# Attention and a cosine-gated feed-forward on one core: the second product for two batches at a time by Strassen's scheme

## The chip, the cores and the metric

The kernel runs on one core of one Trainium2 chip. The metric is the device time of one execution in microseconds (us); shown is the median of several runs. One execution was also taken by the hardware profiler, and all the views of the profile below come from that one.

## The reference

```
q_n, k_n = rmsnorm(q, g_q), rmsnorm(k, g_k)
scores = q_n @ k_n^T / sqrt(64)
attn = softmax(scores)                     # 8 batches, 12 heads, 448 x 448
x = (attn @ v) as 3584 tokens x 768        # 448 tokens of each batch
h = x @ w_in                               # 768 -> 2048
g = h * cos(h)
out = g @ w_out                            # 2048 -> 768
```

Everything is float32 but the two weights, which arrive as float64 and are turned into float32 on the chip. Products are taken at more than the precision of one pass: each operand is split into a high part that TensorE's fast 32-bit format holds (`F32R`) and a low part, the rest, and a product is hi*hi + hi*lo + lo*hi, three matmuls.

## The kernel before

All work is cut into small parts: a Python function that issues a few instructions on one engine. `Plan.add` records a part with its engine, an assumed cost, a due time and the keys it reads and writes; `Plan.order` simulates the five engines' queues with these costs, picks on each engine the ready part with the earliest due time, and so writes out one fixed order. On the chip each engine works through its own instructions in that order and waits on semaphores for the others. There are two plans, one behind the other.

**The first plan** holds the attention of all 8 batches (6 pairs of heads each), the first product (`ffn1`, L478) of batches 0 to 6 laid between, and the decoding of both weights. The first product writes h to DRAM (`h_out` L497, `h_store` L501). The second weight is handled by `weights2` (L606) in 32 halves of 128 x 384: fetched by SP (`v_fetch`), turned from float64 by four instructions of VectorE and one of ScalarE (`decode`, L204), split into high part (ScalarE, L256) and low part (GpSimd, L258), and stored to the scratch tensor `wo_d` in DRAM (`v_store`).

**The second plan** (from L737) has two kinds of work for TensorE. First come the 16 blocks of batch 7's first product (`ffn1_block`), each of 18 matmuls. As each of them ends, the slot of its weight in SBUF takes one row block of the second weight (`v_place`, L265). Then comes the second product of batches 0 to 7 (`ffn2`, L548): 16 steps a batch, a step being one row block of 128 of w_out for six output tiles of 128 x 448, so 6 x 3 = 18 matmuls of 128 x 128 by 128 x 448. The six outputs of a batch build up in six of the eight banks of PSUM.

The operand g of the second product is made for two row blocks at a time, as tiles of 128 x 896 floats, 8 groups a batch and 64 in all. For each of them

- SP loads h from DRAM (`gl_load`, L509),
- VectorE counts turns, h/2pi + a rounding constant (L516), and GpSimd makes the multiple to be subtracted (L518),
- VectorE reduces h in two steps (L524, L526),
- ScalarE takes the absolute value and the sine (L530, L531),
- VectorE multiplies by h (L535),
- ScalarE casts the high part (L544), and GpSimd subtracts it to get the low part (L542).

All their operands lie in SBUF. The rings of buffers are 4 (h), 2 (turns), 2 (reduced), 3 and 3 (high and low parts). At the end of a batch, ScalarE and VectorE copy the six outputs out of PSUM in turn (L568, L570), and SP stores them (`y_store`, L572).

The heart of the second product is

```
nc.tensor.matmul(y, whi, hi, start=(fc == 0), stop=False)
nc.tensor.matmul(y, whi, lo, start=False, stop=False)
nc.tensor.matmul(y, wlo, hi, start=False, stop=(fc == NFC - 1))
```

Of the kernel before, what the change touches and what calls it, by code (L numbers as in the profile page):

```python
# [126 lines left out]
def tile_attention_moe(  # L127
# [108 lines left out]
    half = {}  # L236

    def v_fetch(fc, hf):
        cs = slice(hf * HM, hf * HM + HM)
        st = apool.tile([128, DM], I32, tag="wf", name=f"rawo{fc}_{hf}", bufs=RING["wf"])  # L240
        f = apool.tile([128, DM], F32, tag="wf", name=f"wo{fc}_{hf}", bufs=RING["wf"])
        half[(fc, hf)] = (st, f[:, :HM])
        if f64:
            nc.sync.dma_start(st, w_out[fc][:, cs].bitcast(I32))
        else:
            nc.sync.dma_start(f[:, :HM], w_out[fc][:, cs])

    def v_decode(fc, hf, step):
        st, f = half[(fc, hf)]
        if f64:  # L250
            decode(st, f, step)

    def v_split(fc, hf, lo):
        st, f = half[(fc, hf)]
        if not lo:
            nc.scalar.copy(st.bitcast(F32R)[:, :HM], f)  # L256
        else:
            nc.gpsimd.tensor_tensor(st.bitcast(F32R)[:, HM:], f, st.bitcast(F32)[:, :HM], ALU.subtract)  # L258
# [246 lines left out]
    gts = {}  # L505

    def gl_load(b, gi):
        hb = gpool.tile([128, NG, S], F32, tag="hb", name=f"hb{b}_{gi}", bufs=4)
        nc.sync.dma_start(hb, h_d[b, gi * NG : gi * NG + NG].rearrange("f p s -> p f s"))  # L509
        gts[(b, gi)] = {"h": hb}  # L510

    def g_turns(b, gi, step):
        d = gts[(b, gi)]
        if step == 0:
            n = d["n"] = gpool.tile([128, NG, S], F32, tag="n", name=f"n{b}_{gi}", bufs=2)
            nc.vector.tensor_scalar(n, d["h"], 1.0 / (2.0 * math.pi), MAGIC, op0=ALU.mult, op1=ALU.add)  # L516
        else:
            nc.gpsimd.tensor_scalar(d["n"], d["n"], -MAGIC, -C1, op0=ALU.add, op1=ALU.mult)  # L518

    def g_reduce(b, gi, step):  # L520
        d = gts[(b, gi)]
        if step == 0:
# [1 line left out]
            nc.vector.tensor_tensor(r, d["h"], d["n"], ALU.add)  # L524
        else:
            nc.vector.scalar_tensor_tensor(d["r"], d.pop("n"), C2 / C1, d["r"], op0=ALU.mult, op1=ALU.add)  # L526

    def g_cos(b, gi):
        r = gts[(b, gi)]["r"]
        nc.scalar.activation(r, r, AF.Abs)  # L530
        nc.scalar.activation(r, r, AF.Sin, bias=halfpi, scale=-1.0)  # L531

    def g_mul(b, gi):
        d = gts[(b, gi)]
        nc.vector.tensor_tensor(d["r"], d["r"], d.pop("h"), ALU.mult)  # L535

    def g_split(b, gi, lo):
        d = gts[(b, gi)]
        t = gpool.tile([128, NG, S], F32R, tag="glo" if lo else "ghi", name=f"g{lo}{b}_{gi}")
        d["lo" if lo else "hi"] = t  # L540
        if lo:
            nc.gpsimd.tensor_tensor(t, d.pop("r"), d["hi"].bitcast(F32), ALU.subtract)  # L542
        else:
            nc.scalar.copy(t, d["r"])  # L544

    ys = {}

    def ffn2(b, fc):  # L548
        d = gts[(b, fc // NG)]
        hi, lo = d["hi"][:, fc % NG, :], d["lo"][:, fc % NG, :]  # L550
        w = wts[("wo", fc)]
        for oc in range(NOC):
            if fc == 0:
                ys[(b, oc)] = ps_y.tile([128, 512], F32, tag="y", name=f"y{b}_{oc}")
            y = ys[(b, oc)][:, :S]
            whi = w[:, 0, oc * 128 : oc * 128 + 128]
            wlo = w[:, 1, oc * 128 : oc * 128 + 128]
            nc.tensor.matmul(y, whi, hi, start=(fc == 0), stop=False)  # L558
            nc.tensor.matmul(y, whi, lo, start=False, stop=False)  # L559
            nc.tensor.matmul(y, wlo, hi, start=False, stop=(fc == NFC - 1))  # L560

    yes = {}

    def y_out(b, oc):
        y = ys.pop((b, oc))[:, :S]
        ye = yes[(b, oc)] = xpool.tile([128, S], F32, tag=f"xf{oc}", name=f"ye{b}_{oc}")
        if oc % 2 == 0:
            nc.scalar.copy(ye, y)  # L568
# [37 lines left out]
    def weights2(fc, hf):  # L606
        i = 2 * fc + hf
        d = base(2 * NP) + i * (base(NU - NP // 2) - base(2 * NP)) / (2.0 * NFC)
        st, f = ("wf", NFC + 2 * i), ("wf", NFC + 2 * i + 1)
        add(SP, ISS, d - 20.0, v_fetch, fc, hf, w=[st, f], land=LAND, start=d - 30.0)  # L610
        if f64:
            for step, eng, cost in ((0, DVE, 0.42), (1, DVE, 0.7), (2, DVE, 0.7), (3, ACT, 0.56), (4, DVE, 0.66)):
                add(eng, cost, d + step, v_decode, fc, hf, step,
                    r=[st] if step != 3 else [], w=[f] if step != 3 else [st])
        add(ACT, 0.5, d + 8.0, v_split, fc, hf, False, r=[f], w=[st])
        add(POOL, 1.0, d + 10.0, v_split, fc, hf, True, r=[f], w=[st])
        add(SP, ISS, d + 14.0, v_store, fc, hf, r=[st], land=LAND)
# [119 lines left out]
    RING2 = {"he": 2, "hb": 4, "n": 2, "r2": 2, "ghi": 3, "glo": 3, "y": 8}  # L737
    gpool = ctx.enter_context(tc.tile_pool(name="gpool", bufs=3, reuse_waits="tile"))
    ps_y = ctx.enter_context(tc.tile_pool(name="ps_y", bufs=8, space=PSUM, reuse_waits="tile"))
# [10 lines left out]
    for b in range(B):  # L750
        for gi in range(NFC // NG):
            n = (NFC // NG) * b + gi
            d = BLOCK * (NFC * (b + 1) + NG * gi)
            hb, t, r2, hi, lo = (("hb", n), ("n", n), ("r2", n), ("ghi", n), ("glo", n))
            add(SP, ISS, d - 30.0, gl_load, b, gi, r=[("hd", b, NG * gi + i) for i in range(NG)], w=[hb], land=LAND)
            add(DVE, 0.9, d - 20.0, g_turns, b, gi, 0, r=[hb], w=[t])
            add(POOL, 1.3, d - 19.0, g_turns, b, gi, 1, w=[t])
            add(DVE, 1.1, d - 17.0, g_reduce, b, gi, 0, r=[hb, t], w=[r2])
            add(DVE, 1.8, d - 16.0, g_reduce, b, gi, 1, r=[t], w=[r2])
            add(ACT, 2.0, d - 14.0, g_cos, b, gi, w=[r2])  # L760
            add(DVE, 1.12, d - 11.0, g_mul, b, gi, r=[hb], w=[r2])
            add(ACT, 0.95, d - 9.0, g_split, b, gi, 0, r=[r2], w=[hi])
            add(POOL, 2.8, d - 8.0, g_split, b, gi, 1, r=[r2, hi], w=[lo])
# [58 lines left out]
```

## Time and profile before

| What | us |
|---|---|
| median of 3 runs | 1551.31 (1550.73 to 1553.91) |
| span of the profiled execution, first to last instruction | 1548.5 |
| TensorE busy in it | 1458.9 |
| VectorE busy | 1071.5 |
| ScalarE busy | 884.5 |
| GpSimd busy | 878.3 |

The page gives the span of the profiled execution, and the runs' times include what lies around a span: the median is 2.8 us above it. PE is TensorE's matmuls, PEld its weight loads, DVE VectorE, ACT ScalarE, POOL GpSimd and SP the queue that issues the DMAs. A row of a group gives line, engine, operation, output and inputs, shape and count, then the busy time in us and the mean duration in ns, then the idle time of the engine in front of these instructions and what ended it. Matmuls are pipelined: one shows some 365 ns from start to end, but the next starts 0.2 us behind it, and their busy time counts overlapping ones once. Time in which an instruction waits for a shared resource after it has started counts as busy.

### The profile page before, as it was taken

Reading aid. Unit: us, or ns where it says so; the run is one execution under the profiler, and the core shown is the slowest. Engines: PE = TensorE matmul, PEld = TensorE weight load, DVE = VectorE, ACT = ScalarE, POOL = GpSimd, SP = SyncE. Lnnn points to the kernel's source line nnn. Section 1 sums busy time; section 2 is a strip of 40 time slices with the busy share of each in tenths; the row PEclk is TensorE's granted clock in tenths of the full one; section 3 lists DMA queues with packets and bytes.
Section 4 is the critical chain, followed back from the end, with each engine's and each line's share of the span. In section 5 each row is a group of like instructions: output and inputs, shape, how many; then the busy total and the mean of one; then the engine's idle time right before and its main releaser. Section 6 shows DMA issues by size and latency. Waiting matters only on the chain.

```text
span 1548.5 us, 22570 instructions
## 1 busy us (share of the span) xinstructions
PE 1458.9 (94%) x7680; PEld 1236.1 (80%) x7680; DVE 1071.5 (69%) x1915; ACT 884.5 (57%) x1786; POOL 878.3 (57%) x727
## 2 busy tenths in 40 slices
PE   2777998999999999989999999999999999999999
PEld 1545777778778888878888788889999999999998
DVE  6788998877877777777777775433566666666661
ACT  4676776677776766766676576433344344344341
POOL 7767785876665766665576463141454444444441
PEclk9998999999999999999999999999999999999999
DMA  5436743465545555435454442169133232232220
GB/s 171 126 101 201 221 152 92 129 196 168 175 145 166 161 161 162 154 124 164 142 175 138 133 128 78 47 215 331 48 95 96 71 96 95 72 95 96 72 72 36
DMA packets 118435, 205.26 MB, mean 133 GB/s; under 512 B 19680, under 2 KB 97840, under 8 KB 118320
## 3 DMA queue, kind: packets, MB, share of 16 engines
q1 hardware_dynamic: 118320, 203.82, 42.2%
q8 instruction: 60, 0.98, 0.3%
q14 instruction: 55, 0.45, 0.1%
HBM read 150.47 MB, written 53.30 MB: 132 GB/s over the span
## 4 chain that ended last, share of the span: by engine, by line
PE 77%; DVE 10%; ACT 4%; issue 3%; POOL 1%; DMA 1%; ACTq 0%; SPq 0%; DVEq 0%; POOLq 0%
PE y L558 10%; PE y L560 10%; PE y L559 10%; PE O L444 9%; PE ph L487 8%; PE ph L488 8%; PE ph L489 8%; PE PT L417 8%; PE S L370 6%; ACT hi L424 2%; DVE lo L432 2%; DVE S L377 1%; DVE xf L459 1%; DVE hi L434 1%; DVE wo L212 1%
## 5 line engine op out<-in xcount | busy, mean ns | idle before, releaser
L487 PE MATMUL ph<-xs,wi 128*128 128x448 f32 x768 | 301.2, 392 | 4.6 <-ACT he L499 4.5
L488 PE MATMUL ph<-xs,wi 128*128 128x448 f32 x768 | 283.8, 370 | 1.4 <-POOL xs L473 1.4
L489 PE MATMUL ph<-xs,wi 128*128 128x448 f32 x768 | 283.1, 369 | 0.0
L558 PE MATMUL y<-g,wo 128*128 128x448 f32 x768 | 281.0, 366 | 0.0
L560 PE MATMUL y<-g,wo 128*128 128x448 f32 x768 | 280.5, 365 | 0.0
L559 PE MATMUL y<-g,wo 128*128 128x448 f32 x768 | 280.5, 365 | 0.0
L390 ACT ACTIVATE P<-S,sm 128x448 f32<-128x448 f32 x336 | 214.3, 641 | 98.7 <-DVE S L377 88.1
L424 ACT CAST hi<-PT 128x448 fp32r<-128x448 f32 x384 | 188.2, 536 | 105.8 <-PE PT L417 49.9
L542 POOL TENSOR_TENSOR g<-r,g 128x896 fp32r<-128x896 f32 x64 | 139.7, 2183 | 183.1 <-ACT g L544 183.1
L377 DVE TENSOR_SCALAR_CACHE_REDUCE S<-S,nr 128x448 f32<-128x448 f32 x336 | 219.3, 683 | 20.2 <-PE S L370 18.3
L432 DVE TENSOR_TENSOR lo<-PT,hi 128x448 fp32r<-128x448 f32 x288 | 166.2, 617 | 85.4 <-ACT hi L424 84.3
L417 PE MATMUL PT<-ident,P 128*128 128x128 f32 x1344 | 185.9, 280 | 0.8 <-ACT P L390 0.8
L417 PEld LDWEIGHTS PT<-ident,P 128*128 128x128 f32 x1344 | 163.3, 144 | 17.8 <-issue 3.0
L487 PEld LDWEIGHTS ph<-xs,wi 128*128 128x128 f32 x768 | 146.1, 190 | 34.8 <-issue 12.4
L488 PEld LDWEIGHTS ph<-xs,wi 128*128 128x128 f32 x768 | 146.4, 191 | 12.2 <-POOL xs L473 3.2
L489 PEld LDWEIGHTS ph<-xs,wi 128*128 128x128 f32 x768 | 145.7, 190 | 13.0 <-POOL wi L233 0.4
L444 PE MATMUL O<-hi,vs 128*128 128x448 f32 x384 | 133.5, 398 | 22.7 <-DVE hi L434 9.9
L558 PEld LDWEIGHTS y<-g,wo 128*128 128x128 f32 x768 | 144.2, 188 | 12.9 <-ACT ye L568 0.7
L560 PEld LDWEIGHTS y<-g,wo 128*128 128x128 f32 x768 | 144.3, 188 | 11.4
L559 PEld LDWEIGHTS y<-g,wo 128*128 128x128 f32 x768 | 144.3, 188 | 11.2
L524 DVE TENSOR_TENSOR r<-hb,n 128x896 f32<-128x896 f32 x64 | 93.1, 1455 | 85.4 <-POOL g L542 81.5
L293 POOL TENSOR_TENSOR r<-r,nhalf 128x14 f32<-128x14 f32 (+1 forms) x49 | 127.7, 2606 | 42.0 <-DVE r L289 37.0
(69 smaller groups left out, 2500.0 us busy)
## 6 DMA issues: line engine op xcount, KB each, us to landing
h_d<-he SPq DMA_DIRECT2D x128, 224.0 KB
hb<-h_d SPq DMA_DIRECT2D x64, 448.0 KB
sd<-sd SPq DMA_DIRECT2D x48, 448.0 KB
vd<-v SPq DMA_DIRECT2D x96, 160.0 KB
qd<-qT SPq DMA_DIRECT2D x48, 256.0 KB
raw<-w_in SPq DMA_DIRECT2D x16, 768.0 KB
rawo<-w_out SPq DMA_DIRECT2D x32, 384.0 KB
wo_d<-rawo SPq DMA_DIRECT2D x32, 384.0 KB
```

The source lines that it names most:

```text
L377: nc.vector.tensor_scalar(d["S", t][:, :S], d["S", t][:, :S], d["nr"][:, t : t + 1], None, op0=ALU.mult, op1=ALU.min, accum_out=d["sm"][:, ...
L390: nc.scalar.activation(tl(u, f"P{t}", [128, S], F32, "P"), d.pop(("S", t))[:, :S], AF.Exp, bias=sm[:, 1, t : t + 1], scale=-1.0, accum_out ...
L417: nc.tensor.transpose(pt[:, t * 128 : t * 128 + 128], src, ident)
L424: nc.scalar.copy(hi, pt[:, hh * S : hh * S + S])
L432: nc.vector.tensor_tensor(lo, src, hi.bitcast(F32), ALU.subtract)
L444: nc.tensor.matmul(O, st, d.pop((what, kb, hh)), start=(kc + n == 0), stop=(kc + n == 4))
L487: nc.tensor.matmul(ph[:, :S], whi, x2[:, 0, :], start=(cc == 0), stop=False)
L488: nc.tensor.matmul(ph[:, :S], whi, x2[:, 1, :], start=False, stop=False)
L489: nc.tensor.matmul(ph[:, :S], wlo, x2[:, 0, :], start=False, stop=(cc == NCC - 1))
L558: nc.tensor.matmul(y, whi, hi, start=(fc == 0), stop=False)
L559: nc.tensor.matmul(y, whi, lo, start=False, stop=False)
L560: nc.tensor.matmul(y, wlo, hi, start=False, stop=(fc == NFC - 1))
```

## The change

Take the second weight as a 2 x 2 block matrix (halves of its 2048 rows, halves of its 768 columns) and g of two batches as a 2 x 2 block matrix too (two batches, halves of the 2048 features). The eight block products of the two batches become seven, in the form of Strassen's scheme by Winograd, each a product of one sum of blocks of g and one sum of blocks of the weight.

In the first plan the four quarters belonging to one row block are decoded, VectorE makes four block sums (`v_sum`), and seven factors instead of four are split and stored:

```diff
-    wo_d = dpool.tile([NFC, 128, 2, DM], F32, tag="wo_d", name="wo_d")
+    wo_d = dpool.tile([7, NFC // 2, 128, 2, HM], F32, tag="wo_d", name="wo_d")
...
+        if j == 0:
+            nc.vector.tensor_tensor(temp[(c, 0)], a21, a22, ALU.add)
+        elif j == 1:
+            nc.vector.tensor_tensor(temp[(c, 1)], temp[(c, 0)], a11, ALU.subtract)
+        elif j == 2:
+            nc.vector.tensor_tensor(a21, a11, a21, ALU.subtract)
+        else:
+            nc.vector.tensor_tensor(a11, a12, temp[(c, 1)], ALU.subtract)
...
+        if not lo:
+            part[(c, p)] = apool.tile([128, 2, HM], F32R, tag="ao", name=f"ao{c}_{p}", bufs=RING["ao"])
+            nc.scalar.copy(part[(c, p)][:, 0], f)
+        else:
+            w = part[(c, p)]
+            nc.gpsimd.tensor_tensor(w[:, 1], f, w.bitcast(F32)[:, 0], ALU.subtract)
```

In the second plan the tiles of g get fixed places, four quarters of four tiles (`gq`, A, B, C, D). They are made as before, except that ScalarE counts the turns, and VectorE then forms the sums of quarters in place. A product has four groups; a group is one split tile of g, two row blocks of a factor and three banks, again 18 matmuls:

```diff
+            nc.scalar.activation(gns[i], gq[(q, g)], AF.Copy, bias=MAGIC, scale=1.0 / (2.0 * math.pi))
...
+    def g_sum(dst, a, c, g):
+        nc.vector.tensor_tensor(gq[(dst, g)], gq[(a, g)], gq[(c, g)], ALU.subtract)
...
+    def w_place(i, p, c):
+        slot, k = divmod(i, 2)
...
+        nc.sync.dma_start(wq[slot].bitcast(F32)[:, k], wo_d[p, c])
...
+    def o_copy(bank, dst):
+        nc.scalar.copy(outs["t"][:, dst], banks[bank][:, :S])
+
+    def o_add(bank, src, dst):
+        nc.vector.tensor_tensor(outs["t"][:, dst], banks[bank][:, :S], outs["t"][:, src], ALU.add)
...
+    RING2 = {"he": 2, "n": 2, "r2": 2, "ghi": 4, "glo": 4}
...
+    PRODUCTS = (
+        ("P1", A, 0, "X", True, False), ("P5", A, 8, "Q", True, True), ("P6", A, 16, "Y", True, False),
+        ("P2", Dq, 8, "X", False, True), ("P7", Bq, 24, "Y", False, False), ("P3", C, 8, "Z", True, True),
+        ("P4", Dq, 8, "Y", False, True),
+    )
+    KEEP = ("P1", "P6", "P7")
...
+        produce(A, b0, 0, DUE["P1"])
+        produce(Bq, b1, 0, DUE["P5"])
+        produce(C, b1, HF, DUE["P6"])
+        produce(Dq, b0, HF, DUE["P2"])
...
+            if name == "P1":
+                combine(A, Bq, A, DUE["P5"])
+            elif name == "P5":
+                combine(Bq, C, Bq, DUE["P7"])
+                combine(A, C, A, DUE["P6"])
+            elif name == "P2":
+                combine(Dq, Dq, A, DUE["P4"])
```

The third entry of a product is the first of its eight positions among 32 half slots of weights. The factors of P1, P6 and P7 stay in SBUF for all four pairs of batches; those of P5, P2, P3 and P4 are loaded into the same eight positions in turn, once a pair. P1 and P2 build up in the same banks, and so do P6, P7 and P4. Of the 21 output additions of a pair (7 products, three tiles each), 6 are copies by ScalarE and 15 are additions by VectorE of one operand in PSUM and one in SBUF. The tiles of the attention output (`xf`) move from a pool that lasts for the whole kernel to the first plan's, and the reserve of SBUF for descriptors is set to 1024.

More of the change, by code (lines that the diff above doesn't have):

```diff
@@ L233, in w_low, with v_fetch @@
         eng.tensor_tensor(w[:, 1, cs], wfl[fc][:, cs], w.bitcast(F32)[:, 0, cs], ALU.subtract)
[L236 to L242, printed above, removed]
+    stage, quad, temp, part = {}, {}, {}, {}
+    QUADS = ((0, 1), (1, 1), (0, 0), (1, 0))
+    def v_fetch(c, k):
+        fh, oh = QUADS[k]
+        src = w_out[c + fh * (NFC // 2)][:, oh * HM : oh * HM + HM]
@@ L243, in v_fetch @@
         if f64:
-            nc.sync.dma_start(st, w_out[fc][:, cs].bitcast(I32))
-        else:
[L246 to L254, printed above, removed]
+            st = stage[(c, k)] = apool.tile([128, DM], I32, tag="wf", name=f"rawo{c}_{k}", bufs=RING["wf"])
+            nc.sync.dma_start(st, src.bitcast(I32))
+        else:
+            v_quad(c, k)
+            nc.sync.dma_start(quad[(c, k)], src)
@@ new lines, in v_quad, with v_decode, v_sum @@
+    def v_quad(c, k):
+        quad[(c, k)] = apool.tile([128, HM], F32, tag="aq", name=f"aq{c}_{k}", bufs=RING["aq"])
+    def v_decode(c, k, step):
+        if step == 0:
+            v_quad(c, k)
+        decode(stage[(c, k)], quad[(c, k)], step)
+    def v_sum(c, j):
+        if j < 2:
+            temp[(c, j)] = apool.tile([128, HM], F32, tag="at", name=f"at{c}_{j}", bufs=RING["at"])
+        a21, a22, a11, a12 = (quad.get((c, k)) for k in range(4))
+        if j == 0:
[6 more added lines that the diff above has]
+            nc.vector.tensor_tensor(a11, a12, temp[(c, 1)], ALU.subtract)
@@ L270, in tile_attention_moe, with v_store @@
+    def v_store(c, p):
+        nc.sync.dma_start(wo_d[p, c], part.pop((c, p)).bitcast(F32))
     pair = {}
@@ L502, in h_store, with gl_load @@
         nc.sync.dma_start(h_d[b, fc], hes.pop((b, fc)))
[L505 to L513, printed above, removed]
+    NGR = NFC // 2 // NG
+    gq, gns, grs, gsp = {}, {}, {}, {}
+    def gl_load(b, q, g, f0):
+        nc.sync.dma_start(gq[(q, g)], h_d[b, f0 : f0 + NG].rearrange("f p s -> p f s"))
@@ L546, in tile_attention_moe @@
[L546 to L560, printed above, removed]
@@ new lines, in ffn2 @@
+    def ffn2(n, g, wpos, bank3, opens):
+        first, last = opens and g == 0, g == NGR - 1
+        hi, lo = gsp.pop((n, 0)), gsp.pop((n, 1))
+        for e in range(NG):
+            slot, k = divmod(wpos[e], 2)
+            w = wq[slot][:, k]
+            for o in range(3):
+                y = banks[bank3[o]][:, :S]
+                whi, wlo = (w[:, j, o * 128 : o * 128 + 128] for j in range(2))
+                more = {"skip_group_check": not opens}
+                nc.tensor.matmul(y, whi, hi[:, e], start=first and e == 0, stop=False, **more)
+                nc.tensor.matmul(y, whi, lo[:, e], start=False, stop=False, **more)
+                nc.tensor.matmul(y, wlo, hi[:, e], start=False, stop=last and e == NG - 1, **more)
@@ L604, in weights @@
             add(POOL, 1.15, d, w_low, fc, hf, nc.gpsimd, r=[f, w], w=[("wlo", fc, hf)])
[L606 to L617, printed above, removed]
+    SPLITS = (("P2", 3, 2), ("P4", 1, 2), ("P1", 2, 3), ("P5", 4, 3), ("P6", 5, 4), ("P7", 0, 5), ("P3", 2, 6))
@@ new lines, in tile_attention_moe, with weights2 @@
+    PRODUCT = {"P1": 0, "P5": 1, "P6": 2, "P2": 3, "P7": 4, "P3": 5, "P4": 6}
+    def weights2(c):
+        span = (base(NU - NP // 2) - base(2 * NP)) / (NFC / 2.0)
+        d = base(2 * NP) + c * span
+        qk = [("aq", 4 * c + k) for k in range(4)]
+        tk = [("at", 2 * c + j) for j in range(2)]
+        for k in range(4):
+            st, f, e = ("wf", NFC + 4 * c + k), qk[k], d + 0.1 * span * k
+            if f64:
+                add(SP, ISS, e - 20.0, v_fetch, c, k, w=[st], land=LAND, start=e - 30.0)
+                for step, eng, cost in ((0, DVE, 0.42), (1, DVE, 0.7), (2, DVE, 0.7), (3, ACT, 0.56), (4, DVE, 0.66)):
+                    add(eng, cost, e + step, v_decode, c, k, step,
+                        r=[st] if step != 3 else [], w=[f] if step != 3 else [st])
+            else:
+                add(SP, ISS, e - 20.0, v_fetch, c, k, w=[f], land=LAND, start=e - 30.0)
+        sums = (
+            (0, qk[0:2], [tk[0]]), (1, [tk[0], qk[2]], [tk[1]]),
+            (2, [qk[2]], [qk[0]]), (3, [qk[3], tk[1]], [qk[2]]),
+        )
+        made = {"P2": 0, "P4": 0, "P1": 0, "P5": 1, "P6": 2, "P7": 3, "P3": 4}
+        done = 0
+        for n, (name, src, _) in enumerate(SPLITS):
+            e = d + span * (0.4 + 0.08 * n)
+            p = PRODUCT[name]
+            while done < made[name]:
+                j, r, w = sums[done]
+                add(DVE, 0.55, e - 6.0, v_sum, c, j, r=r, w=w)
+                done += 1
+            f = tk[src - 4] if src > 3 else qk[src]
+            o = ("ao", 7 * c + n)
+            add(ACT, 0.5, e, v_split, c, p, src, False, r=[f], w=[o])
+            add(POOL, 1.0, e + 2.0, v_split, c, p, src, True, r=[f], w=[o])
+            add(SP, ISS, e + 5.0, v_store, c, p, r=[o], land=LAND)
@@ L712, in multiply @@
                 r += [("xs", cc, s) for cc in (2 * part, 2 * part + 1) for s in range(2)]
-                add(PE, 1.215, d, ffn1, b, fc, part, ps_h, "ph", r=r, w=[key])
+                add(PE, 1.215, d, ffn1, b, fc, part, r=r, w=[key])
             add(ACT, 0.53, d - 4, h_out, b, fc, r=[key], w=[("he", NFC * b + fc)])
@@ L728, in tile_attention_moe @@
             multiply(b)
-    for i in range(2 * NFC):
-        weights2(*divmod(i, 2))
+    for c in range(NFC // 2):
+        weights2(c)
     with tc.manual_schedule():
@@ L734, in tile_attention_moe @@
     att.close()
[L737 to L739 removed]
+    RING2 = {"he": 2, "n": 2, "r2": 2, "ghi": 4, "glo": 4}
+    gpool = ctx.enter_context(tc.tile_pool(name="gpool", bufs=1, reuse_waits="tile"))
+    ps_y = ctx.enter_context(tc.tile_pool(name="ps_y", bufs=1, space=PSUM, reuse_waits="tile"))
+    banks = [ps_y.tile([128, 512], F32, tag=f"y{i}", name=f"y{i}") for i in range(8)]
+    for q in range(4):
+        for g in range(NGR):
+            gq[(q, g)] = gpool.tile([128, NG, S], F32, tag=f"g{q}_{g}", name=f"gq{q}_{g}")
     plan = Plan(RING2)
@@ L750, in tile_attention_moe @@
[L750 to L763, printed above, removed]
-            for fc in (NG * gi, NG * gi + 1):
-                out_keys = [("y", NFC + NOC * b + oc) for oc in range(NOC)]
-                add(PE, BLOCK, BLOCK * (NFC * (b + 1) + fc), ffn2, b, fc, r=[hi, lo, ("w", fc)], w=out_keys)
-        for oc in range(NOC):
-            y = ("y", NFC + NOC * b + oc)
-            d = BLOCK * NFC * (b + 2) + oc
-            add(DVE if oc % 2 else ACT, 0.62 if oc % 2 else 0.53, d - 12.0, y_out, b, oc, r=[y], w=[("ye", oc)])
-            add(SP, ISS, d, y_store, b, oc, r=[("ye", oc)], land=LAND)
@@ new lines, in tile_attention_moe @@
+    add(ACT, 0.05, BLOCK * NFC + 4.0, o_tile, r=[("y", i) for i in range(8)], w=[("o", i) for i in range(12)])
+    A, Bq, C, Dq = range(4)
+    PRODUCTS = (
+        ("P1", A, 0, "X", True, False), ("P5", A, 8, "Q", True, True), ("P6", A, 16, "Y", True, False),
+        ("P2", Dq, 8, "X", False, True), ("P7", Bq, 24, "Y", False, False), ("P3", C, 8, "Z", True, True),
+        ("P4", Dq, 8, "Y", False, True),
+    )
+    KEEP = ("P1", "P6", "P7")
+    free = list(range(8))
+    n_split = 0
+    placed = {}
```

157 lines of the change are left out of this document (110 added, 47 removed).

## The prediction

> **What bounds the kernel now.** I read the page's header and chain of waits first, then the table of busy time by stretch, then the groups by line, and last the order of time on VectorE and GpSimd.
>
> ```profile
> span 1548.5 us, 22570 instructions
> ...
> PE 77%; DVE 10%; ACT 4%; issue 3%; POOL 1%; DMA 1%; ACTq 0%; SPq 0%; DVEq 0%; POOLq 0%
> ```
> ```profile
> 280.00:1000.00 720.00, 704.43 (x3935) 579.68 (x3935) 532.58 (x1174) 488.34 (x1135) 438.43 (x408) 0.99 0.48 146
> 1039.46:1058.40 18.94, 18.94 (x96) 17.54 (x95) 15.54 (x13) 9.30 (x13) 10.13 (x5) 1.00 1.00 362
> 1082.00:1540.00 458.00, 458.00 (x2259) 423.27 (x2258) 275.56 (x255) 179.71 (x200) 208.43 (x118) 1.00 0.25 77
> ```
> ```profile
> L558 PE MATMUL y<-g,wo x768: 360/365/472, 1077.2 to 1544.2; 128*128 128x448 f32 x192
> L560 PE MATMUL y<-g,wo x768: 362/365/369, 1077.6 to 1544.6; 128*128 128x448 f32 x192
> ```
>
> Columns of the middle fence: stretch and length, then busy time of PE, PEld, DVE, ACT, POOL, granted clock, DMA share, GB/s. The second product runs from 1077.2 to 1544.6 plus one 0.2 us pitch: 467.6 us for 128 steps (8 batches x 16 rows of w_out), 18 matmuls and 3.65 us a step. PE is busy all 458 us of its stretch. So the stage is bound by PE, and a cut of one step in eight there looks worth 16 x 3.65 = 58.4 us. Stage one is PE's too, nearly: 704 of 720 us.
>
> VectorE shows 275.6 us busy there and GpSimd 208.4, which together exceed 458. Whether these two really run side by side decides this case:
>
> ```profile
> 1042.15 2.85 POOL L542 TENSOR_TENSOR g<-r,g 128x896 fp32r<-128x896 f32 x1 [0.26 <-ACT g L544]
> 1050.27 3.06 POOL L542 TENSOR_TENSOR g<-r,g 128x896 fp32r<-128x896 f32 x1 [2.68 <-ACT g L544]
> 1053.97 1.64 POOL L518 TENSOR_SCALAR n<-n 128x896 f32<-128x896 f32 x1 [0.65 <-DVE n L516]
> ```
> ```profile
> 1043.05 2.90 DVE L526 SCALAR_TENSOR_TENSOR r<-n,r 128x896 f32<-128x896 f32 x1
> ...
> 1050.24 1.09 DVE L526 SCALAR_TENSOR_TENSOR r<-n,r 128x896 f32<-128x896 f32 x1
> 1051.25 2.56 DVE L516 TENSOR_SCALAR n<-hb 128x896 f32<-128x896 f32 x1
> 1053.73 1.08 DVE L535 TENSOR_TENSOR r<-r,hb 128x896 f32<-128x896 f32 x1
> ```
> ```profile
> L524 DVE TENSOR_TENSOR r<-hb,n x64: 1079/1452/1825, 1013.5 to 1512.6; 128x896 f32<-128x896 f32 x64
> L526 DVE SCALAR_TENSOR_TENSOR r<-n,r x64: 1083/1092/2899, 1014.6 to 1513.7; 128x896 f32<-128x896 f32 x64
> L518 POOL TENSOR_SCALAR n<-n x64: 937/1637/1677, 1012.5 to 1505.0; 128x896 f32<-128x896 f32 x64
> L542 POOL TENSOR_TENSOR g<-r,g x64: 2116/2136/3057, 1036.0 to 1524.2; 128x896 fp32r<-128x896 f32 x64
> L459 DVE TENSOR_TENSOR xf<-O,xf x96: 579/622/629, 56.9 to 1007.7; 64x448 f32<-64x448 f32 x96
> ```
>
> They don't. L542 began at 1050.27, just after L526 had started (it ended at 1051.33), and ended 2.00 us after that end. L516 issued meanwhile and ended at 1053.81, 0.48 us after L542. L535 ended 1.00 us later (1054.81), L518 0.80 us after L535. The L526 of 2.90 us ended 0.95 us behind L542. Each instruction waits for the other engine's. The L524 rows say it in bulk: 1.08 us at least, 1.82 at most. L459, whose one operand is in PSUM, shows no such spread (579 to 629 ns). So VectorE's SBUF-only work and GpSimd's form **one queue**, with holds, when they alternate, of about 2.00 (L542), 0.80 (L518), 1.00 (L524, L526, L535) and 0.48 us (L516); alone the first three cost 2.14, 0.94 and 1.09. Before, a group of two steps (7.3 us of PE) needs 2.00 + 0.80 + 3 x 1.00 + 0.48 = 6.28 us of that queue, 86%. PE is the bound by one seventh only.
>
> **The change, part by part.**
>
> PE. A pair of batches takes 7 products x 4 groups = 28 groups of 18 matmuls in place of 32. The matmul's shape stays, so 112 x 3.65 = 409.2 us: -58.4 if PE stays fed.
>
> The shared queue. The work to produce g stays: 16 tiles a pair (64 in all, as now), each with L518's subtraction and three two-input VectorE instructions.
> - Removed: L516's 0.48 us, which goes to ScalarE. There it costs about what L530 does, 64 x 0.95 us; ScalarE was busy 180 of 458 us, and becomes busy for 16 x 2.95 + 28 x 0.94 + 6 x 0.53 = 77 us a pair. Hidden.
> - Added: 16 sums a pair, 128x896 with two SBUF operands, priced as L535.
> - Added: splits of all seven factors, 28 a pair instead of 16: 12 more of L542 on GpSimd (and of L544 on ScalarE, counted above).
> - The output additions read PSUM: 15 x 0.62 us a pair on VectorE alone, as L459.
>
> ```profile
> L544 ACT CAST g<-r 128x896 fp32r<-128x896 f32 x64 | 60.2, 940 | 142.9 <-PE y L560 137.1 <-DVE r L524 3.4 <-DVE r L535 2.2
> L531 ACT ACTIVATE r<-r,halfpi 128x896 f32<-128x896 f32 x64 | 66.9, 1046 | 2.1
> L530 ACT ACTIVATE r<-r 128x896 f32<-128x896 f32 x64 | 60.9, 952 | 118.4 <-DVE r L526 118.3
> L568 ACT COPY ye<-y 128x448 f32<-128x448 f32 x24 | 11.9, 533 | 28.2 <-PE y L560 28.2
> ```
>
> Per pair: 28 x 2.00 + 16 x 0.80 + 64 x 1.00 = 132.8 us with every hold shortened by alternation, 144.8 us by the lone durations. PE needs 102.3 us. The queue becomes the bound, and four pairs hold it 531 to 579 us against 467.6 for the whole stage now.
>
> The Trainium skill, in "SBUF — State Buffer", section "Who interferes with whom", says that a VectorE instruction with two SBUF inputs and a GpSimd instruction reading SBUF exclude each other for the whole instruction; its paragraph on the bandwidth pool has the loser begin some 115 ns after the winner's end. By that rule lone durations add in full, and the estimate for a pair would be some 155 us, the whole near 1680 us; the rows above show the loser ending earlier than its lone duration instead, so I go by the rows.
>
> When the queue is needed. Tiles of g live in place: A is free for the next pair when D has been overwritten by D-A (at P2), B after P7's splits, C after P3's, D after P4's. So the next pair is produced during P7, P3, P4, and the following P1 and P5. Those five products hold the queue for 20 x 2.00 + 16 x 0.80 + 52 x 1.00 = 104.8 us against 73 of PE. P6 and P2 hold 8 splits and 12 sums, 28 us, PE 29.2.
>
> How full the queue runs: from 1039.46 to 1058.40 it held 9 x 1.00 + 3 x 0.80 + 2 x 2.00 + 4 x 0.48 = 17.3 of 18.9 us (VectorE x13, GpSimd x5), 91%; the gaps were waits on ScalarE that the added sums can fill. Between 91 and 100% I take 95%: 110.3 us for the five products, 30 for the two.
>
> First pair. It is produced under batch 7's first product, as soon as the last x_split is through:
>
> ```profile
> 1013.89 8.05 POOL L473 TENSOR_TENSOR xs<-xf,xs 128x448 fp32r<-128x448 f32 x6 [0.44 <-ACT xs L471]
> ```
>
> From 1022 to 1077 there are 55 us; 16 tiles and 4 splits hold 16 x 3.80 + 8 = 68.8 us, 72.4 at 95%. The 17.4 left join 12 splits and 16 sums (42.1): 59.5 beside PE's 58.4. With both so near I take 62. Last pair: behind P2 nothing is produced, PE's 12 groups of P7, P3 and P4 set 43.8 us.
>
> Stage two: 62 + 3 x (110.3 + 30) + 43.8 = 526.7, **+59.1 us** against 467.6.
>
> Waits and queues. A VectorE addition into the output now waits for its product on PE; queued behind it are the next quads' reductions, for which ScalarE waits. SP's store of an output waits for that addition, and the loads of later quads stand behind it. A bubble of 3 us at each of 28 products would be 84 us, none would be 0; by the plan's order the production for a product is emitted before its addition, so I take none beyond the 5%. The weights of P3 and P4 follow each other in the same slots, a load of two 384 KB halves having about 11 us. Traffic is 12.6 + 7.3 + 2.8 = 22.7 MB a pair, 162 GB/s over 140 us, where 362 was seen: no bound. The end (last matmul to last store) stays at 3.7 us.
>
> Stage one. 32 more sums of 128x384 on VectorE (as L218), 24 more casts and 24 more subtractions, 24 more stores on SP:
>
> ```profile
> L258 POOL TENSOR_TENSOR rawo<-wo,rawo 128x384 fp32r<-128x384 f32 x32 | 32.4, 1012 | 39.2 <-ACT rawo L256 39.2
> L218 DVE SCALAR_TENSOR_TENSOR wo<-rawo,wo 128x384 f32<-128x384 f32 x32 | 19.8, 617 | 0.1
> L256 ACT CAST rawo<-wo 128x384 fp32r<-128x384 f32 x32 | 16.5, 514 | 4.7 <-DVE wo L218 4.2
> ```
> ```profile
> PE 1458.9 (94%) x7680; PEld 1236.1 (80%) x7680; DVE 1071.5 (69%) x1915; ACT 884.5 (57%) x1786; POOL 878.3 (57%) x727
> ```
>
> That is 19.7, 12.3 and 24.3 us. VectorE has 10% of the chain's span (155 of its 1071 us busy, 14%), ScalarE 7% and GpSimd 2% likewise: 2.8 + 0.9 + 0.4 = +4.1. Ends: 0 (or a gain of 1, since raw staging and floats no longer share a ring), and +20 if all sums show.
>
> Sum: 1548.5 + 59.1 + 4.1 = 1611.7 us of span. The runs' median lies 2.8 above that span: **1614.5, say 1615 us**.
>
> **Rivals.**
> 1. *PE stays the bound* (faster). Place: the queue of VectorE and GpSimd in stage two. If their instructions overlapped, VectorE would need 16 x 3.27 + 16 x 1.09 + 9.3 = 79 and GpSimd 75 us of 102, and the time would be 1551.3 - 58.4 + 4 = 1497. It decides from the point where the 108 holds of a pair fall under 102.3 us, 0.95 us each against 1.23 measured. For it: each engine alone has room. Against: the rows of L524 and L542. 9%.
> 2. *The queue packs perfectly*, production drifting from the five products into the two: 1022 + 531 + about 12 of PE-only end + 3.7, plus 2.8, is 1572. 15% for 1560 to 1590.
> 3. *Stalls by order*: additions at the head of VectorE's queue, or the lone durations (114.5 / 0.91 = 126 us for the five products, 33 for the two), give 1615 + 3 x 19 = 1672. 11%.
> 4. *PE's clock falls*, since PE will wait in most groups.
> ```profile
> 120.00:140.00 20.00, 15.85 (x69) 10.82 (x68) 16.39 (x34) 11.63 (x29) 14.59 (x14) 0.76 0.61 197
> ```
> With PE busy 79%, the granted clock was 0.76: a group would take 4.8 us, still under the 5.5 that the queue takes in the five products, and the two products lose 9 us a pair. At half clock the five would take 146: 1615 + 3 x (36 + 28) = 1807. 7%, mostly at the mild end (1640). The Trainium skill, "TensorE: Matmul & The Clock Gate", Part 1, puts the clock back to half after an idle window of about 3.4 us. By that rule it hangs on single gaps of PE, which I expect near 2 us.
> 5. *Nothing measurable changes*: 3%, gains and costs meeting.
>
> **How the numbers follow.** Forecast 55% (1590 to 1645), rival 1 9%, rival 2 15%, rival 3 11%, rival 4 7%, rival 5 3%. A measurement here tells apart about 0.2%. Faster 0.09, same 0.03, slower 0.88. The range is 1560 to 1670: it leaves out rivals 1 and 5 and about half of 3 and 4.
>
> **What would show it.** Right: PE under 80% busy from 1090 to 1500, medians of the sums and of L524 and L526's successors well over 1.09 us, GpSimd's splits often over 2.14, and PE waiting for GpSimd's split. In P6, P2 and at the very end PE should be full. Wrong: PE at 100% throughout, or PE waiting for weights or h by DMA, or stage one ending over 15 us later.

## The result, and the profile after

The changed kernel takes 1624.15 us (median of 4 runs, 1620.0 to 1625.43) against 1552.61 before: 1.0458 times as long, 95% interval 1.0435 to 1.0481. The forecast was 1615, slower. The profiled execution has a span of 1618.2 us, 69.7 more than before.

First the rows of TensorE's second product (minimum, median and maximum duration in ns, then first and last start), and busy time by stretch in the columns of the prediction:

```profile
L576 PE MATMUL y<-g,wo x672: 360/368/742, 1066.6 to 1613.9; 128*128 128x448 f32 x168
L578 PE MATMUL y<-g,wo x672: 358/368/575, 1067.0 to 1614.3; 128*128 128x448 f32 x168
```
```profile
280.00:1000.00 720.00, 704.69 (x3975) 584.43 (x3975) 548.46 (x1213) 499.99 (x1165) 469.96 (x434) 1.00 0.51 159
...
1085.00:1570.00 485.00, 380.97 (x1725) 333.25 (x1726) 428.30 (x267) 241.98 (x278) 341.53 (x150) 0.92 0.47 154
...
1291.70:1431.50 139.80, 111.33 (x506) 96.86 (x505) 128.44 (x80) 71.85 (x83) 100.05 (x44) 0.93 0.49 163
...
1570.80:1614.50 43.70, 43.70 (x217) 40.34 (x215) 4.67 (x8) 8.99 (x11) 19.10 (x9) 1.00 0.43 135
```

The product now runs from 1066.6 to 1614.5: 547.9 us against 467.6, although it has an eighth fewer matmuls. It begins 10.6 us earlier than before. So stage one got shorter and stage two 80.3 us longer. PE is busy 381 of 485 us there; VectorE shows 428 and GpSimd 342, together 770 in 485 us: time in which one waits for the other is in it, as the next rows show.

The instructions of the two engines after (the first four rows give minimum, median and maximum, the last two busy time and mean):

```profile
L554 POOL TENSOR_TENSOR g<-gq,g x112: 2092/2788/3079, 1036.7 to 1601.2; 128x896 fp32r<-128x896 f32 x112
...
L535 DVE TENSOR_TENSOR r<-gq,n x64: 1076/1094/3030, 1014.6 to 1537.6; 128x896 f32<-128x896 f32 x64
L545 DVE TENSOR_TENSOR gq<-r,gq x64: 1077/1812/3030, 1020.8 to 1542.3; 128x896 f32<-128x896 f32 x64
L548 DVE TENSOR_TENSOR gq<-gq,gq x64: 1072/1094/3026, 1053.3 to 1559.6; 128x896 f32<-128x896 f32 x64
```
```profile
L537 DVE SCALAR_TENSOR_TENSOR r<-n,r 128x896 f32<-128x896 f32 x64 | 118.4, 1851 | 1.6
...
L530 POOL TENSOR_SCALAR n<-n 128x896 f32<-128x896 f32 x64 | 102.8, 1606 | 56.4 <-ACT n L528 44.2 <-DVE r L535 5.2 <-DVE gq L548 3.1
```

The minima are what they were (1.08 us on VectorE, 2.1 for the low part), and the maxima are that plus the other engine's instruction: 3.03 and 3.08. The low part's median rose from 2.14 to 2.79 us.

Where the time goes within a pair is read from the order of the matmuls, 72 to a product. Start to start, in us:

```
pair   P1    P5    P6    P2    P7    P3    P4    sum
1     24.0  22.8  23.4  14.6  14.6  16.2  19.9  135.6
2     23.1  19.6  31.9  14.9  14.9  15.1  19.9  139.5
3     23.2  19.6  32.1  14.9  14.9  15.0  20.0  139.7
4     21.6  21.1  32.0  14.6  14.6  14.6  14.6  133.1
```

At full rate a product takes 14.6. Pairs 2 and 3 repeat to 0.2 us. From P7 to P7 (the row 1291.70 to 1431.50, with 44 instructions on GpSimd, and 80 on VectorE of which 15 are output additions) the queue was held 28 x 2.00 + 16 x 0.80 + 64 x 1.00 = 132.8 us by the prediction's holds, of 139.8: 95%. The starts and ends in the trace say the same: one of the two engines is inside such an instruction for 132.0 of that period's 139.7 us. TensorE was busy 79% from 1085 to 1570. P6 takes 32 us for a reason of its own, seen in the order of time of pair 3, on VectorE, GpSimd and TensorE:

```profile
1395.03 2.95 DVE L545 TENSOR_TENSOR gq<-r,gq 128x896 f32<-128x896 f32 x1
1397.90 1.08 DVE L535 TENSOR_TENSOR r<-gq,n 128x896 f32<-128x896 f32 x1
1399.01 1.09 DVE L537 SCALAR_TENSOR_TENSOR r<-n,r 128x896 f32<-128x896 f32 x1
1400.02 1.68 DVE L589 TENSOR_TENSOR outs<-y,outs 128x448 f32<-128x448 f32 x3
...
1403.62 1.08 DVE L548 TENSOR_TENSOR gq<-gq,gq 128x896 f32<-128x896 f32 x1
1408.81 1.09 DVE L548 TENSOR_TENSOR gq<-gq,gq 128x896 f32<-128x896 f32 x1 [4.11 <-POOL g L554]
```
```profile
1391.37 5.66 POOL L554 TENSOR_TENSOR g<-gq,g 128x896 fp32r<-128x896 f32 x2
1406.65 2.13 POOL L554 TENSOR_TENSOR g<-gq,g 128x896 fp32r<-128x896 f32 x1 [9.62 <-ACT g L556]
```
```profile
1400.69 0.74 PE L576 MATMUL y<-g,wo 128*128 128x448 f32 x1 [12.70 <-DVE outs L589]
1401.23 0.57 PE L577 MATMUL y<-g,wo 128*128 128x448 f32 x1
...
1405.34 0.44 PE L576 MATMUL y<-g,wo 128*128 128x448 f32 x1
1405.62 0.37 PE L577 MATMUL y<-g,wo 128*128 128x448 f32 x1
```

P6 opens three banks, and the third of them is one of P5's (nine are wanted, there are eight). P5's additions into the output stand in VectorE's queue behind its backlog of reductions, and until 1400 PE waits for them, 12.7 us. Meanwhile the four buffers for high parts stay full: ScalarE's next cast must wait for PE, GpSimd waits 9.6 us for that cast, and VectorE 4.1 us for GpSimd. From 1404.70 to 1406.65 neither of the two does anything. That is the longest stop of the shared queue in the period, and it is only 1.95 us: while PE waits, the queue mostly works on.

### The profile page after: what moved, and what is told of

It reads as the page before. It is cut to its first block, busy times and chain, and to the rows that moved or that the text cites. A ratio compares the mean times of both kernels' runs of the same rounds, so it can differ in the third digit from the quotient of the medians.

```text
span 1618.2 us, 22760 instructions
## 1 busy us (share of the span) xinstructions
PE 1423.6 (88%) x7392; PEld 1190.8 (74%) x7392; DVE 1270.4 (79%) x1983; ACT 986.5 (61%) x1922; POOL 1076.2 (67%) x799
## 5 line engine op out<-in xcount | busy, mean ns | idle before, releaser
L554 POOL TENSOR_TENSOR g<-gq,g 128x896 fp32r<-128x896 f32 x112 | 289.1, 2586 | 143.7 <-ACT g L556 133.4
L576 PE MATMUL y<-g,wo 128*128 128x448 f32 x672 | 254.1, 378 | 61.7 <-DVE outs L589 44.8
L577 PE MATMUL y<-g,wo 128*128 128x448 f32 x672 | 256.2, 381 | 46.0 <-POOL g L554 45.9
L501 PE MATMUL ph<-xs,wi 128*128 128x448 f32 x672 | 264.7, 394 | 3.0 <-ACT he L513 2.8
L578 PE MATMUL y<-g,wo 128*128 128x448 f32 x672 | 251.6, 374 | 0.0
L502 PE MATMUL ph<-xs,wi 128*128 128x448 f32 x672 | 247.9, 369 | 0.0
L503 PE MATMUL ph<-xs,wi 128*128 128x448 f32 x672 | 247.4, 368 | 0.0
L576 PEld LDWEIGHTS y<-g,wo 128*128 128x128 f32 x672 | 130.5, 194 | 78.8 <-DVE outs L589 46.3
L577 PEld LDWEIGHTS y<-g,wo 128*128 128x128 f32 x672 | 130.5, 194 | 70.1 <-POOL g L554 59.0
L541 ACT ACTIVATE r<-r 128x896 f32<-128x896 f32 x64 | 61.0, 953 | 187.5 <-DVE r L537 187.4
L556 ACT CAST g<-gq 128x896 fp32r<-128x896 f32 x112 | 104.2, 934 | 89.2 <-PE y L578 72.0
L458 PE MATMUL O<-hi,vs 128*128 128x448 f32 x384 | 135.0, 399 | 25.4 <-DVE hi L448 10.6
L501 PEld LDWEIGHTS ph<-xs,wi 128*128 128x128 f32 x672 | 127.7, 190 | 29.9 <-issue 10.9
L548 DVE TENSOR_TENSOR gq<-gq,gq 128x896 f32<-128x896 f32 x64 | 112.8, 1769 | 40.8 <-POOL g L554 40.8
L535 DVE TENSOR_TENSOR r<-gq,n 128x896 f32<-128x896 f32 x64 | 119.0, 1859 | 32.7 <-POOL n L530 30.4
```

The source lines that it names most:

```text
L501: nc.tensor.matmul(ph[:, :S], whi, x2[:, 0, :], start=(cc == 0), stop=False)
L502: nc.tensor.matmul(ph[:, :S], whi, x2[:, 1, :], start=False, stop=False)
L503: nc.tensor.matmul(ph[:, :S], wlo, x2[:, 0, :], start=False, stop=(cc == NCC - 1))
L554: nc.gpsimd.tensor_tensor(t, gq[(q, g)], gsp[(n, 0)].bitcast(F32), ALU.subtract)
L576: nc.tensor.matmul(y, whi, hi[:, e], start=first and e == 0, stop=False, **more)
L577: nc.tensor.matmul(y, whi, lo[:, e], start=False, stop=False, **more)
```

## The experiments

The theory is that of the prediction: VectorE's instructions with two operands in SBUF and GpSimd's that read SBUF hold one queue, and its holds set stage two. The rivals: G, GpSimd's own occupation; V, VectorE's own work; Q, output additions late in VectorE's order, holding PSUM banks.

**GpSimd writes only.**

```diff
-            nc.gpsimd.tensor_tensor(t, gq[(q, g)], gsp[(n, 0)].bitcast(F32), ALU.subtract)
+            for _ in range(2):
+                nc.gpsimd.memset(t.bitcast(F32), 1e-4)
```

> GpSimd writes a constant into the low parts of g, twice over, in place of subtracting (the low parts of g are left out of the result). Its instructions stay, but they read no SBUF. Theory (VectorE and GpSimd share one queue for SBUF reads): a pair holds that queue 64 x 1.00 + 16 x 0.80 = 76.8 us, under PE's 102, so PE bounds stage two again: about 1500 us (1480 to 1520), and the VectorE instructions fall back to near 1.09 us. Rival G (GpSimd's own occupation is the bound): no change, 1600 or more. Rival V (VectorE's own work is the bound, it shows 98% busy): no change either.

Measured: 1486.37 us, a single run. Busy time by stretch, and VectorE's rows:

```profile
1085.00:1480.00 395.00, 395.00 (x1941) 365.88 (x1940) 271.87 (x267) 247.57 (x281) 240.06 (x263) 0.99 0.61 202
```
```profile
L535 DVE TENSOR_TENSOR r<-gq,n x64: 1074/1084/1095, 1012.7 to 1404.4; 128x896 f32<-128x896 f32 x64
L545 DVE TENSOR_TENSOR gq<-r,gq x64: 1076/1091/1826, 1018.9 to 1410.6; 128x896 f32<-128x896 f32 x64
L548 DVE TENSOR_TENSOR gq<-gq,gq x64: 1072/1084/1824, 1048.3 to 1423.3; 128x896 f32<-128x896 f32 x64
```

PE is full. GpSimd is still busy 61% of the stretch, and VectorE gets through 267 instructions in 272 us, as many as the changed kernel's stretch shows with 428: 156 us of its "busy" time there were waiting. The maxima of 1.82 us that are left belong to the turns, which still read. V falls. G isn't excluded by this run alone, since the two writes take 1.70 us where the subtraction took 2.59.

The Trainium skill, "SBUF — State Buffer", section "Who interferes with whom", says just this: a two-input VectorE instruction contends with a GpSimd instruction that reads SBUF and not with one that only writes it. This run agrees.

**Low parts on VectorE.**

```diff
-            nc.gpsimd.tensor_tensor(t, gq[(q, g)], gsp[(n, 0)].bitcast(F32), ALU.subtract)
+            nc.vector.tensor_tensor(t, gq[(q, g)], gsp[(n, 0)].bitcast(F32), ALU.subtract)
...
-                add(POOL, 2.2, e - 8.0, g_split, n, q, g, 1, r=[("G", q, g), hk], w=[lk])
+                add(DVE, 1.1, e - 8.0, g_split, n, q, g, 1, r=[("G", q, g), hk], w=[lk])
```

> VectorE makes the low parts of g, all else as in the changed kernel; GpSimd keeps only the turns. Theory: a low part holds the shared queue 1.0 us instead of 2.0, so a pair holds it 92 x 1.00 + 16 x 0.80 = 105.6 us instead of 132.8, about PE's 102: stage two falls by some 90 us, 1530 us (1505 to 1550), although VectorE gets 112 more instructions. Rival V (VectorE is the bound by its own work): 112 x 1.09 = 122 us more on it, 1700 or more. Rival G: about 1500.

Measured: 1532.82 us, 0.9871 of the kernel before (0.9845 to 0.9896). The engine that showed 88% busy was given 112 more instructions, and the kernel got some 90 us shorter:

```profile
1085.00:1520.00 435.00, 405.61 (x1904) 366.51 (x1905) 387.04 (x380) 255.22 (x287) 59.82 (x51) 0.96 0.55 184
```
```profile
L554 DVE TENSOR_TENSOR g<-gq,g x112: 1072/1083/1830, 1040.8 to 1514.9; 128x896 fp32r<-128x896 f32 x112
```

The same subtraction holds the queue half as long on VectorE (1.08 us against 2.09 at least). V is refuted here as well. G would have freed PE as wholly as the writes did (about 1500); the theory's 1530 came, with the holds near PE's need, 105.6 against 102. That the sum fits is partly luck. From P7 to P7 only the first period runs at the pace of the holds (105.2 us). The next two take 119.5 and 119.3, of which the two engines' instructions fill 106 to 107; there P6 waits 6.2 us for P5's additions, and some low parts come late.

**No sums.** The call in `combine` is left out.

> The 64 sums of quarters of g are left out (the products take the quarters themselves). Theory: 16 holds of 1.00 us less a pair, and the wait of a sum for the split before it goes too: 1560 to 1580 us. Rival Q (PE is held by output additions that stand late in VectorE's queue and keep a bank of PSUM, whatever the queue's holds): the additions stay, so at most 20 us less, 1605.

Measured: 1551.17 us, a single run. Some 73 us less, more than the 64 holds of 1.00 us are worth: P6 falls to 14.9 us in every pair, since without the sums P5's additions come in time as well. Q's bound of 20 us is far off. The period from P7 to P7 of pair 3 against the changed kernel's 139.8:

```profile
1264.90:1383.10 118.20, 109.66 (x506) 98.22 (x506) 97.90 (x63) 71.71 (x82) 96.00 (x45) 0.96 0.55 191
```

No matmul of the second product waits for an output addition here, GpSimd has the same instructions as in the changed kernel, and PE's own work is 102 us. Yet a pair takes 118.2 us, for 28 x 2.00 + 16 x 0.80 + 48 x 1.00 = 116.8 us of holds; by starts and ends the queue is in use for 116.8 of them. So G is refuted (its work didn't change, and the pair lost 21 us), and the holds set the pace without any help from Q.

**P2 before P6**: the same holds, with a product between P5 and P6, so that P6 should find its bank empty.

```diff
-        ("P1", A, 0, "X", True, False), ("P5", A, 8, "Q", True, True), ("P6", A, 16, "Y", True, False),
-        ("P2", Dq, 8, "X", False, True), ("P7", Bq, 24, "Y", False, False), ("P3", C, 8, "Z", True, True),
+        ("P1", A, 0, "X", True, False), ("P5", A, 8, "Q", True, True), ("P2", Dq, 8, "X", False, True),
+        ("P6", A, 16, "Y", True, False), ("P7", Bq, 24, "Y", False, False), ("P3", C, 8, "Z", True, True),
```

> The changed kernel with the products in the order P1, P5, P2, P6, P7, P3, P4: P6 no longer opens a bank right behind P5, whose output addition still has to empty it (that wait held PE 12.7 us once a pair). Theory of the shared queue: holds stay 132.8 us a pair where a pair takes 139.7, so at most 7 us a pair go, 1600 to 1624. Rival Q (the wait for the addition sets the pace): 12.7 us go in each of three pairs and some 7 in the first, about 1580.

Measured: 1602.83 us, 1.0332 of before (1.0311 to 1.0352). By the matmuls' order, P1 to P1 takes 134.8 and 135.1 us in pairs 2 and 3, where it took 139.5 and 139.7. But PE's wait for additions did not go, it moved. In pair 3:

```profile
1404.43 0.47 PE L576 MATMUL y<-g,wo 128*128 128x448 f32 x1 [1.77 <-DVE outs L589]
...
1428.30 0.71 PE L576 MATMUL y<-g,wo 128*128 128x448 f32 x1 [10.21 <-DVE outs L589]
```

The first row is P6's third bank. The second is P7, which builds up on P6's banks and now follows it at once, before VectorE has added P6's result. Together that is 12.0 us (12.6 from P7 of pair 1 to P7 of pair 2), nearly the 12.7 of the changed kernel. So the 1580 of rival Q, for a kernel rid of the wait, was not put to the test. What the run does show is that PE waits as long for additions and the pair is still 5 us shorter: the time in which neither engine uses the queue fell from 7.7 us to 3.5 between two P7, and the pair now lies 2 us above the 132.8 of the holds. It is the queue's idle time that costs, and not PE's wait.

**Late first loads.** The first pair's 16 loads of h, each at most 60 us ahead of its due time:

```diff
-                    w=[k], land=LAND)
+                    w=[k], land=LAND, start=max(0.0, e - 60.0) if t == 0 else 0.0)
```

> The changed kernel with the first pair's loads of h started in steps, nothing else. In the trace after, the 16 loads at once hold back the stores of batch 7's h, ScalarE waits for those with its copies, and the first pair's reductions start some 15 us late; P1 to P7 of the first pair take 84.9 us where 62 were predicted. If that is the cause: 10 to 20 us less, 1604 to 1614. If the queue of the first pair is full anyway: 1624.

Measured: 1611.84 us, 1.0373 (1.0348 to 1.0397). The stretch ahead of the first product, in the changed kernel and with late loads:

```profile
1020.00:1065.00 45.00, 45.00 (x224) 41.69 (x223) 31.39 (x21) 25.26 (x33) 21.87 (x11) 1.00 0.84 303
```
```profile
1020.00:1065.00 45.00, 45.00 (x223) 41.70 (x223) 41.52 (x30) 31.76 (x42) 26.04 (x13) 1.00 0.96 333
```

VectorE gets 30 instructions done instead of 21, and P1 to P7 of the first pair takes 75.0 us instead of 84.9. ScalarE's waits for stores of h between 1015 and 1068 fell from 10.1 us to 1.5.

**Stage one alone**: the new first plan with the old second plan (its weights loaded as two pieces of `wo_d` each).

> The first plan of the changed kernel with the second plan of the kernel before (its weights are taken from four of the seven stored factors, so the second product is that of other weights). By the step of the prediction: 4 us slower than before, 1556. By the two traces, in which the second product begins 10.6 us earlier after the change: 1542.

Measured: 1543.29 us, 0.9944 (0.9922 to 0.9966): 8 to 9 us shorter, and not 4 longer.

**An own ring** in the kernel before, for the floats of w_out (and, as after the change, a reserve of 1024 for descriptors, whose share in the result is not shown apart):

```diff
-        f = apool.tile([128, DM], F32, tag="wf", name=f"wo{fc}_{hf}", bufs=RING["wf"])
+        f = apool.tile([128, HM], F32, tag="aq", name=f"wo{fc}_{hf}", bufs=RING["aq"])
```

> The kernel before, with the one edit that raw halves of w_out and their floats no longer share a ring of two buffers (as in the changed kernel). If that sharing is why stage one was longer before: 1542, as with the whole first plan of the change. If the gain comes from elsewhere (fewer and other due times, other order): 1551.

Measured: 1548.19 us, 0.9979 (0.9962 to 0.9996), between the two. The first step of decoding, in the kernel before, with its own ring, and after the change (first and last start behind the durations):

```profile
L210 DVE TENSOR_SCALAR wo<-rawo x32: 342/357/1321, 287.6 to 919.1; 128x384 int32<-128x384 int32 x32
```
```profile
L210 DVE TENSOR_SCALAR wo<-rawo x32: 341/358/1458, 277.1 to 834.5; 128x384 int32<-128x384 int32 x32
```
```profile
L211 DVE TENSOR_SCALAR aq<-rawo x32: 340/354/1304, 280.6 to 802.6; 128x384 int32<-128x384 int32 x32
```

Before, a half took both buffers of the ring, so the next could be fetched only when it was stored, and the decoding dragged on to 919. With its own ring it ends 85 us sooner, after the change 117. By the ratios the sharing explains some 3 of the 9 us (1 to 6 by the interval); what the rest is stays open.

**Versions meant to beat both.** Low parts on VectorE, late loads, and P2 before P6:

> Low parts on VectorE, P2 before P6, and the first pair's loads of h started in steps (each at most 60 us ahead of its due time in the plan) instead of all at once. Theory: the holds of 105.6 us a pair stay near PE's 102, the first pair's delay (some 20 us) and the waits for P5's addition (16 us in all) mostly go: 1505 (1495 to 1520). If neither mattered: 1530 as with the low parts alone.

Measured: 1535.13 us, 0.9898 (0.9878 to 0.9918), a miss: no better than the low parts alone. The first pair is repaired (P1 to P7 60.4 us), but pairs 2 to 4 lose some 15 us each at P2, where PE stands 8 and 4 us in front of the first group, for its high and its low part. P2 now needs D one product earlier, and D is the quarter that is freed and made last. Which of the two makes it late is not shown.

The same with both steps of the turns on ScalarE:

```diff
-            nc.gpsimd.tensor_scalar(gns[i], gns[i], -MAGIC, -C1, op0=ALU.add, op1=ALU.mult)
+            nc.scalar.activation(gns[i], gns[i], AF.Copy, bias=-MAGIC, scale=1.0)
...
-            nc.vector.tensor_tensor(r, gq[(q, g)], gns[i], ALU.add)
+            nc.vector.scalar_tensor_tensor(r, gns[i], -C1, gq[(q, g)], op0=ALU.mult, op1=ALU.add)
...
-            nc.vector.scalar_tensor_tensor(grs[i], gns.pop(i), C2 / C1, grs[i], op0=ALU.mult, op1=ALU.add)
+            nc.vector.scalar_tensor_tensor(grs[i], gns.pop(i), -C2, grs[i], op0=ALU.mult, op1=ALU.add)
```

> The same, and both steps of the turns on ScalarE, so that GpSimd does nothing in stage two. The queue is then VectorE's alone: 92 x 1.00 + 9.3 = 101 us a pair, ScalarE has 92 us. Theory: PE bounds, 1495 (1485 to 1510). If ScalarE's chain becomes the bound: 1510 to 1530.

Measured: 1521.54 us, 0.9807 (0.9783 to 0.9832), again above the theory's 1510. PE waits at P2 in each later pair, some 3 us for the high part and 5.4 to 5.8 for the low one. The rival named ahead, ScalarE's chain, gives 1510 to 1530 as well, and this run alone doesn't exclude it. So the order was put back, with ScalarE's work as it is here:

> Low parts on VectorE, turns on ScalarE, late first loads, and the products in their order as changed (P6 before P2). With P2 before P6 each of the three later pairs lost 15 us at P2, since D, which P4 frees last, was needed one product earlier. Theory: without that PE bounds, 1500 us (1490 to 1512). If the addition of P5 then holds P6's bank as before (6 us and more once a pair): 1515 to 1525, no better than with the other order.

Measured: **1503.18 us, 0.9672 (0.965 to 0.9693)**, faster than both kernels.

```profile
1085.00:1490.00 405.00, 391.67 (x1897) 359.22 (x1896) 354.23 (x371) 291.91 (x329) 0.00 (x0) 0.98 0.60 197
```

PE is busy 97%, and pairs 1 and 2 run at 102.1 us each, PE's own time. So the order was what cost time, and ScalarE's work is not the bound. The longest waits left are two of P6 for P5's additions, 5.5 us each, in pairs 3 and 4.

Last, the kernel before with its low parts on VectorE:

> The kernel before, with the low parts of g made by VectorE as well, to see whether that move alone is a gain. Theory: the queue had room there (86%), PE is the bound in stage two, so nothing moves: 1552 (1548 to 1556).

Measured: 1552.4 us, 0.9994 (0.9975 to 1.0012), no difference:

```profile
1082.00:1540.00 458.00, 458.00 (x2262) 424.40 (x2261) 306.94 (x316) 183.89 (x200) 53.82 (x57) 1.00 0.25 79
```

PE was full and is full. So the low parts' move by itself is worth nothing; together with Strassen's scheme it makes the scheme pay.

## Why the prediction was right, point by point

- *The bound moves from PE to one queue of VectorE and GpSimd*: right, and shown. Taking GpSimd's reads away left PE full (1486). Leaving out 16 sums brought a pair to 118.2 us for 116.8 of holds. A new order brought it to 135 for 132.8, though PE waited for additions as long as ever. Halving the low part's hold (1533) fits in the sum, but only one of its three later periods ran at the pace of the holds.
- *The later pairs*: 3 x 140.3 = 421 us predicted from P7 to P7, measured 419.3 (1151.5 to 1570.8). *The end*: 43.8 predicted, 43.7 measured.
- *Which products are slow*: wrong in part. I put PE at full rate in P6 and P2; it was so in P2, P7 and P3, and P6 was the slowest. The sum over a pair stood, because it is the queue's total that counts.
- *Waits of output additions*: "none beyond the 5%". One of 12.7 us a pair was there, and another 12.6 us of PE's idle time in pair 3 was spread over ten waits for low parts. They cost little because the queue works on meanwhile: it stood unused 7.7 us of that period in all, which is what the 5% held.
- *The first pair*: 62 us predicted, 84.9 measured, the largest mis-sized term of stage two (+23 of the 21 us by which that stage was missed, the later pairs giving 2 back). What was wrong is that I let the queue be full from 1022 on. But the plan issues all 16 loads of h at once; batch 7's stores wait behind them in the DMA queues, ScalarE's copies wait for their buffers, and with them the turns. Late loads brought 10 us back there; P6's wait for the additions (6.5 us in that run) and low parts that came late (5.0 us) are what else the trace shows.
- *Stage one*: +4.1 predicted, about -9 measured: the step that failed in sign. I priced the added instructions by their share of the chain, and gave the freed ring "a gain of 1" at most. It was worth some 3, and there is a further gain, which the runs didn't place.
- The two errors, +21 and -15 (10.6 earlier instead of 4.1 later), have opposite signs, so that the total was nearer (1615 for 1624) than its terms. That closeness is luck.
- *The signs named ahead*: PE was 79% busy and GpSimd's low parts took 2.79 us in the median, as forecast. The medians of the sums (L548) and of L524's successor (L535) were forecast well over 1.09 us and stayed at 1.09; there the waiting shows in the means, 1.77 and 1.86. The median of L537, as L526 is now, went to 1.71, as forecast.
- *Rival 1*, PE stays the bound: refuted. *Rival 2*, perfect packing: not reached, but the pair with P2 ahead comes within 2 us of it. *Rival 3*: its wait was seen, its price wasn't paid. *Rival 4*, the clock: seen at its mild end (0.92 granted from 1085 to 1570), as shown below.

## What to carry to other kernels

Before trading TensorE work for elementwise work, add up the holds of VectorE instructions with two SBUF operands and of GpSimd instructions that read SBUF as if one engine did them; busy shares of the two that look safe apart (275.6 and 208.4 of 458 us here before the change, 60% and 46%) can be one resource that is nearly full (86%). Then an instruction belongs on the engine where its hold is shorter, even if that engine looks the busier, and a plan that simulates the two engines as independent, as this kernel's does, will not see it. Look also at what a burst of early loads holds back: a store, the buffer it frees, and the engine that fills that buffer next.
